# Moving three loads in a gated attention and mixer kernel: late v pieces of batch 1 at outputs 14 to 22, mixer weights V and U at outputs 11 and 13

## The chip, the cores and the metric

The kernel runs on one core of one Trainium2 chip. The metric is the device time of one execution in microseconds (us). Work is done by five engines with queues of their own: TensorE (PE; its weight loads are shown apart as PEld), VectorE (DVE), ScalarE (ACT), GpSimd (POOL) and SyncE (SP). In this kernel GpSimd and SP mostly issue DMA transfers; 16 DMA engines carry them all.

## The reference

For each of 8 batches (u and v are 3136 x 256, z is 3136 x 64, all float32), attention without softmax, gated by u, and then a mixer with a residual:

```
scores = (z @ z.T) / 3136
attn   = maximum(scores, 0) ** 2
x      = u * (attn @ v)                      # first part: gated attention

h      = x.T @ U @ V                         # U: 3136 x 32, V: 32 x 3136
y      = x + h.T
out    = y + maximum(y @ w_ch1, 0) @ w_ch2   # w_ch1: 256 x 1024, w_ch2: 1024 x 256
```

U, V, w_ch1 and w_ch2 are shared by all batches. The mixer of a batch needs the x of the whole batch.

## The kernel before

The 3136 rows are cut into 25 tiles of up to 128 rows (24 full, one of 64, tile 24). The attention matrix is symmetric, so only half of its blocks are computed: for row tile j, `A[j]` (line 129) holds 13 blocks, those of tiles j to j + 12, counted around. `score` (line 352) makes them: matmuls of z against z (line 359), Relu with the scale on ScalarE (line 372), squaring on VectorE (line 374), in bf16. The other half is had by transposing: `turn` (line 392) issues a DMA transpose on SP (line 394) that turns the 12 later blocks of `A[o]` into a *strip*, one of seven buffers. A strip is called here by its tile.

An *output* is one row tile of attn @ v. `attend_steps` (line 526) makes it: 25 blocks, each as two matmuls of 64 rows (line 472), 13 blocks from the A tiles and 12 from the strip. Outputs go in the order of tiles 12, 13, ... 24, 0, ... 11, and "output i" of a batch is the i-th of these (`turns`, line 132). Two outputs share an accumulator and a load of u (`load_u`, line 452, two buffers); when the second is done, `close_pair` (line 481) adds the halves (lines 486, 487) and multiplies by u on VectorE (line 502). In the first output of a pair, the block of tile 24 is also done for the second output, so the second output's strip is needed already at the end of the first.

Batch 0 begins without any A tile. `start_up` (line 768) makes outputs 0 to 7 in an order of its own: outputs 0 to 3 from blocks made on the spot, outputs 4 to 7 with the strips of tiles 16 to 19. From output 8 (tile 20) on, the main loop (line 957) runs one output after the other, and spreads score steps, for outputs to come and for the next batch, between its matmuls. Strips of batch 0 are issued as `first_turns` (line 920) and `lead` (line 944) say; outputs 17 and 18 of batch 0 (tiles 4 and 5) use two strips that ScalarE and VectorE make without a DMA (`rebuild_steps`, line 397). From batch 1 on the mixer of the batch before runs beside attention: `rank_sums` (line 563) is the first user of U, at output 0 of batch 1; `low_rank` (line 615), the up matmuls (line 654) and the down matmuls (line 701) follow. V is copied by VectorE from a staging place (`V_tmp`, line 120) to its own tile by the `puts` (line 940) at outputs 16 to 21 of batch 0 and at output 0 of batch 1.

The order of every engine's queue is the order in which the program is written: no scheduler moves anything. GpSimd's queue holds all loads that convert float32 to bf16. A GpSimd instruction that waits holds back all that stand behind it; one that has nothing to wait for goes out as soon as the one before it has. So a load that is written "after output 11" goes out when the loads written before it are out, not when output 11 is done.

v is double buffered by batch (`v_both`, line 126). It is loaded in nine pieces (`V_PARTS`, line 311): eight of three tiles, and tile 24. Before the change, batch 1's pieces are placed so: pieces 0 to 2 in the opening, behind w_ch1, U and V (line 796, `run(fetches)`); pieces 3 and 4 in the opening too, behind a one-column copy on GpSimd, `mark` (line 869), which waits for the strip of tile 19 to land; the piece of tile 24 at output 10; pieces 5, 6 and 7 at outputs 17, 20 and 22 (line 955). They are first read at output 0 of batch 1.

Of the kernel before, what the change touches and what calls it, by code (L numbers as in the profile page):

```python
# [8 lines left out]
BF16 = mybir.dt.bfloat16  # L9
# [9 lines left out]
def _spread(main, filler):  # L19

    n, m = len(main), len(filler)
    k = 0
    for i, step in enumerate(main):
        step()
        while k < m and (2 * k + 1) * n <= (i + 1) * 2 * m:
            filler[k]()
            k += 1
    for step in filler[k:]:
        step()


def _merge(*lists):

    keyed = [
        ((i + 0.5) / len(part), n, s)
        for n, part in enumerate(lists)
        for i, s in enumerate(part)
    ]
    return [s for _, _, s in sorted(keyed, key=lambda e: e[:2])]
# [3 lines left out]
def kernel(  # L43
# [11 lines left out]
    nc = tc.nc  # L55

    B, S, D = u.shape
# [3 lines left out]
    P = 128  # L61
# [12 lines left out]
    LEAD = FIRST + AHEAD  # L74
    NG = 4
# [5 lines left out]
    persist = ctx.enter_context(tc.tile_pool(name="persist", bufs=1))  # L81
# [11 lines left out]
    halves = [slice(h * ROWS, (h + 1) * ROWS) for h in range(2)]  # L93


    mark = persist.tile([P, 1], BF16, name="mark")
    sets = [[ps1_pool.tile([P, 512], FP32, name=f"ps{k}{h}") for h in range(2)] for k in range(2)]
    opened = [0]

# [32 lines left out]
    def turns(i):  # L132
        return (FIRST + i) % NT
# [9 lines left out]
    def rows(ap):  # L143
        return ap[: NF * P, :].rearrange("(p t) d -> p t d", t=NF)
# [10 lines left out]
    def bursts_at(b):  # L155

        at = {0: (NC - 1, NC)} if b > 1 else {}
        if b:
            at.update({6: (0, 1, 2), 13: (3, 4, 5)})
        if b == B - 1:  # L160
            at[17] = (NC - 1, NC)
        return at
# [52 lines left out]
    def load_z(b, parts):  # L215
        if b not in z_raw:
            z_raw[b] = stage.tile([P, NT + 1, dqk], BF16, name="z_c")
        z_c = z_raw[b]
        for t0, t1 in parts:
            pool_dma(out=z_c[:, t0:t1, :], in_=rows(z[b])[:, t0:t1, :])  # L220
            if t1 == NF:
                for r in halves:
                    pool_dma(out=z_c[r, NF, :], in_=z[b, NF * P :, :])
# [78 lines left out]
    def load_v(b, part):  # L302
        t0, t1 = part
        v_bf = v_both[b % 2]
        if t0 < NF:
            pool_dma(out=v_bf[:, t0:t1, :], in_=rows(v[b])[:, t0:t1, :])  # L306
        else:
            for r in halves:
                pool_dma(out=v_bf[r, NF, :], in_=v[b, NF * P :, :])

    V_PARTS = [(t, t + 3) for t in range(0, NF, 3)] + [(NF, NT)]
    WHOLE = ((0, NF),)

    def weight_steps():


        def first_w():
            pool_dma(out=w1_bf, in_=moe_w_ch1.rearrange("(t p) d -> p t d", p=P))

        def second_w():  # L320
            pool_dma(out=w2_bf, in_=moe_w_ch2.rearrange("(p t) d -> p t d", t=NH))

        def narrow():
            pool_dma(out=U_bf[:, :NF, :], in_=rows(moe_U))
            pool_dma(out=U_bf[:TAIL, NF, :], in_=moe_U[NF * P :, :])

        def fetch():
            pool_dma(out=V_tmp, in_=moe_V)

        def put(ta, tb):  # L330
            src = V_tmp[:, : NF * P].rearrange("r (p t) -> r t p", t=NF)
            nc.vector.tensor_copy(
                out=V_bf[:R, col(ta) : col(ta) + (tb - ta) * P].rearrange("r (t p) -> r t p", p=P),
                in_=src[:, ta:tb, :],
            )

        def put_tail():
            for c in (col(NF), col(NF) + TAIL):
                nc.vector.tensor_copy(out=V_bf[:R, c : c + TAIL], in_=V_tmp[:, NF * P :])

        def copies(n):
            nc.vector.tensor_copy(out=V_bf[n : 2 * n, :], in_=V_bf[:n, :])

        fetches = [first_w, narrow, fetch]
        third = FIRST // 2
        puts = [lambda t=t: put(t, t + third) for t in range(0, NF, third)]
        return fetches, second_w, puts + [put_tail], [lambda n=n: copies(n) for n in (R, 2 * R)]


    strips = {}  # L350
# [417 lines left out]
    def start_up():  # L768
# [4 lines left out]
            out=eye,  # L773
            in_=eye,
# [18 lines left out]
            load_u(0, o)  # L793
        if B > 1:
            load_z(1, WHOLE)
        run(fetches)
        if B > 1:
            for part in V_PARTS[:3]:
                load_v(1, part)
# [65 lines left out]
            if j <= some[-1]  # L865
        ]
        run(_merge(nxt[2:], own))
        if B > 1:
            nc.gpsimd.tensor_copy(out=mark, in_=strips[0, LEAD + NG - 1][:, 0, :1])
            for part in V_PARTS[3:5]:  # L870
                load_v(1, part)
        rest = [
            lambda pair=pair: make_stored(pair, LEAD + NG)
            for pair in zip(range(LEAD - 1, FIRST - NG, -2), range(LEAD - 2, FIRST - NG - 1, -2))
# [59 lines left out]
    def run(steps):  # L934
        for s in steps:
            s()

    fetches, second_w, puts, copies = weight_steps()
# [9 lines left out]
    for b in range(B):  # L948
        more = b + 1 < B
        begin = 0 if b else 2 * NG  # L950
        all_bursts.append(bursts_of(b))
        burst_at = bursts_at(b)
        v_in = list(V_PARTS) if more and b else []
        own = own_at if b else first_at
        v_at = dict(zip((17, 20, 22, 10), V_PARTS[5:]))
        ahead = dict(zip((2, 3, 4, 7, 10, 11, 14), range(NC)))
        for i in range(begin, NT):
            o = turns(i)
            fill = [s for key in own.get(i, ()) for s in score_steps(b, *key)]
            if b == 0 and i in first_new:  # L960
                fill += rebuild_steps(b, first_new[i])
            if b == 0 and i in first_more:
                fill.append(lambda args=first_more[i]: make_stored(*args))
            if b == 0 and i == begin:
                fill = panel + fill
            if more:
                coming = next_at if b else after_first
                fill += [s for key in coming[i] for s in score_steps(b + 1, *key)]
                if b and i == (1 if b > 1 else 5):
                    load_z(b + 1, WHOLE)  # L970
                if i == (7 if b > 1 else 11 - 2 * b):
                    turn_z(b + 1, (FIRST, NF))
                if i == (10 if b else 12):
                    turn_z(b + 1, (0, FIRST))
                if b == 0 and i == 14:
                    mirror_z((FIRST, NF))
                if i in (16, 18, 20) and v_in:
                    load_v(b + 1, v_in.pop(0))
                if b == 0 and i in v_at:
                    load_v(b + 1, v_at[i])  # L980
                if b == 0 and i == 15:
                    mirror_z((0, FIRST))
                    extend_z(b + 1)
            main = attend_steps(b, o)
            if b and i in ahead:
                at = 17 if (i + (i > FIRST)) % 2 == 0 else 12 if i == 7 else 9 if i == 3 else 10
                main.insert(at, lambda c=ahead[i]: low_rank(b - 1, c))
            _spread(main, fill)
            if b == 0 and i in first_turns:
                for t in first_turns[i]:  # L990
                    turn(b, t)
            else:
                now = b * NT + i
                for k in range(turned_to[0] + 1, min(now + lead(b, i), NT * B - 1) + 1):
                    turn(k // NT, turns(k % NT))
                    turned_to[0] = k
            if not more and i == NT - AHEAD:
                turn_x(b, 0)
            if b * NT + i in puts:
                puts[b * NT + i]()  # L1000
            if (b, i) == ((1, 1) if more or b else (0, 20)):
                second_w()
            if b and i == 0:
                ps = spare()[0]
                rank_sums(b - 1, ps)
                rank_close(b - 1, ps)
            for n in burst_at.get(i, ()):
                up, down = all_bursts[b - 1 if i else b - 2][n]
                if i and not more and n >= NC - 1:
                    late += up + down  # L1010
                    up, down = [], []

                steps = [down.pop(0)] if n == 4 and n == burst_at[i][0] else []
                steps += _merge(up, down)
                if more:
                    steps = _merge(steps, [lambda part=part: load_v(b + 1, part) for part in [v_in.pop(0)]])
                    if n == 3:
                        steps.insert(2, lambda: mirror_z((FIRST, NF)))
                        steps.insert(4, lambda: mirror_z((0, FIRST)))
                        steps.insert(6, lambda: extend_z(b + 1))  # L1020
                run(steps)
# [4 lines left out]
    b = B - 1  # L1026
# [46 lines left out]
```

## Time and profile before

| what | us |
|---|---|
| median of 3 runs | 995.64 |
| lowest and highest of them | 995.33, 1003.48 |
| the profiled execution | 995.98 |
| its span, first to last instruction | 994.3 |
| DVE and ACT busy in the span | 552.7, 615.5 |
| GpSimd busy in the span | 169.5 |
| DMA transposes of strips in the span | 194, of 5.5 from issue to landing (median) |
| loads of v in the span | 57 pieces of 192 KB, 4.5 from issue to landing (median) |

The profile is of one execution. A timeline line gives start, length, engine, line of the kernel, operation, what is written and read, shapes and count, and in brackets how long the engine had been idle and what released it. "SPq" and "POOLq" are the queues that issue DMAs. In the list of DMA issues, "us to landing" is from the issue to the semaphore that tells of the data's arrival.

### The profile page before, as it was taken

To read this page: it belongs to the slowest core of one execution; us is meant where nothing else is said; L and a number is where in the kernel's file an instruction comes from. 1 tells how busy PE (TensorE), PEld (TensorE's weight loads), DVE (VectorE), ACT (ScalarE), POOL (GpSimd) and SP (SyncE) were. 2 spreads that over 40 slices of the span, in tenths; PEclk is the share of its full clock that TensorE was granted. 3 is DMA by queue.
4 is the path that set the end of the run, shared out by engine and by line. 5 is a ranking of instruction groups with operands and counts; after the bars stand their busy time and mean duration, and the time that the engine had idled before them with its cause. 6 is when DMAs were issued, how large, how long until landed. Compare 5 with 4: busy or idle time off the path is not lost.

```text
span 994.3 us, 31019 instructions
## 1 busy us (share of the span) xinstructions
PE 978.9 (98%) x13632; PEld 815.5 (82%) x13672; DVE 552.7 (56%) x1025; ACT 615.5 (62%) x845; POOL 169.5 (17%) x317
## 2 busy tenths in 40 slices
PE   8899999999999999999999999999999999999998
PEld 6778878888788888788887888878888788788876
DVE  6779845567346574364653655546546466352342
ACT  8878764766647575475755757467574676643154
POOL 5111111112121111212112121121211201111000
PEclk9999999999999999999999999999999999999999
DMA  9999999899899998998989989889989796595443
GB/s 180 163 192 209 181 155 202 174 184 174 142 196 175 168 178 151 181 179 169 168 163 172 180 166 169 162 171 186 159 165 185 164 192 125 129 191 122 83 107 101
DMA packets 399976, 164.42 MB, mean 165 GB/s; under 512 B 375568, under 2 KB 384464, under 8 KB 399840
## 3 DMA queue, kind: packets, MB, share of 16 engines
q1 hardware_dynamic: 371520, 96.14, 61.5%
q0 software_dynamic: 28320, 66.28, 28.9%
q8 instruction: 107, 1.75, 0.8%
q14 instruction: 29, 0.24, 0.1%
HBM read 61.88 MB, written 25.69 MB: 88 GB/s over the span
## 4 chain that ended last, share of the span: by engine, by line
PE 95%; DMA 2%; DVE 1%; ACT 1%; issue 0%; POOL 0%; DVEq 0%; POOLq 0%
PE ps L472 51%; PE ps L701 17%; PE ps L654 17%; PE ps L359 7%; DMA strip<-A 1%; PE ps L622 1%; PE ps L512 1%; DMA v<-in_v_dram 1%; ACT A L372 1%; PE ps L567 1%; DVE A L374 0%; DMA out_dram<-o_sb 0%; DVE both L487 0%; ACT both L486 0%; DVE x_bf L502 0%
## 5 line engine op out<-in xcount | busy, mean ns | idle before, releaser
L372 ACT ACTIVATE A<-ps 128x832 bf16<-128x832 f32 (+9 forms) x481 | 358.4, 764 | 141.0 <-PE ps L359 135.6
L472 PE MATMUL ps<-v,A 64*128 64x256 bf16 x4988 | 341.2, 269 | 1.6 <-DVE A L374 1.1
L374 DVE TENSOR_TENSOR A<-A 128x832 bf16<-128x832 bf16 (+9 forms) x481 | 243.5, 523 | 135.4 <-ACT A L372 133.1
L472 PE MATMUL ps<-v,strip 64*128 64x256 bf16 x4420 | 310.3, 269 | 3.8 <-DMA strip<-A 3.0
L472 PEld LDWEIGHTS <-A 64*128 64x128 bf16 x4988 | 252.7, 94 | 40.0 <-issue 7.0
L672 ACT ACTIVATE relu_bf<-ps 128x1024 bf16<-128x1024 f32 (+2 forms) x208 | 188.3, 909 | 150.5 <-PE ps L654 144.7
L472 PEld LDWEIGHTS <-strip 64*128 64x128 bf16 x4420 | 227.6, 94 | 35.0 <-DMA strip<-A 4.6
L701 PE MATMUL ps<-w_bf,relu_bf 128*128 128x256 bf16 (+1 forms) x1600 | 201.4, 273 | 0.4
L654 PE MATMUL ps<-ut,w_bf 128*128 128x512 bf16 (+2 forms) x856 | 198.1, 353 | 1.7
L701 PEld LDWEIGHTS <-relu_bf 128*128 128x128 bf16 (+1 forms) x1600 | 153.0, 98 | 40.3 <-issue 4.9
L719 DVE TENSOR_TENSOR o_sb<-ps,x_bf 128x512 f32<-128x512 f32 (+2 forms) x81 | 54.8, 678 | 171.1 <-PE ps L701 166.1
L654 PEld LDWEIGHTS <-w_bf 128*128 128x128 bf16 x896 | 117.9, 144 | 37.4 <-issue 6.7
L359 PE MATMUL ps<-zT 64*128 64x416 bf16 (+8 forms) x812 | 134.8, 312 | 0.0
L456 POOL DMA_DIRECT2D u_sb<-in_u_dram x96 | 53.1, 554 | 444.4 <-DVE x_bf L502 426.3
L486 ACT COPY both<-ps 128x512 f32<-128x512 f32 (+1 forms) x104 | 59.0, 568 | 70.1 <-PE ps L472 64.0
L487 DVE TENSOR_TENSOR both<-ps,both 128x512 f32<-128x512 f32 (+1 forms) x104 | 69.3, 666 | 30.8 <-ACT both L486 30.2
L502 DVE TENSOR_TENSOR x_bf<-both,u_sb 128x512 bf16<-128x512 f32 (+1 forms) x104 | 69.8, 672 | 3.7
L636 DVE TENSOR_TENSOR x_bf<-ps,x_bf 128x512 bf16<-128x512 f32 (+1 forms) x112 | 65.5, 626 | 11.3 <-PE ps L622 11.2
L732 POOL DMA_DIRECT2D out_dram<-o_sb x66 | 36.1, 546 | 186.4 <-DVE o_sb L719 174.5
L359 PEld LDWEIGHTS <-zT 64*128 64x128 bf16 x812 | 46.3, 94 | 3.6
L719 DVE TENSOR_TENSOR both<-ps,x_bf 128x512 f32<-128x512 f32 (+1 forms) x24 | 15.0, 623 | 57.3 <-PE ps L701 57.3
L306 POOL DMA_DIRECT2D v<-in_v_dram x61 | 33.7, 556 | 3.9 <-issue 2.7
(65 smaller groups left out, 242.8 us busy)
## 6 DMA issues: line engine op xcount, KB each, us to landing
u_sb<-in_u_dram POOLq DMA_DIRECT2D x96, 256.0 KB, 4.2
out_dram<-o_sb POOLq DMA_DIRECT2D x66, 256.0 KB, 2.9
v<-in_v_dram POOLq DMA_DIRECT2D x57, 192.0 KB, 4.5
out_dram<-both POOLq DMA_DIRECT2D x18, 256.0 KB, 2.5
strip<-A SPq DMA_TRANSPOSE x194, 5.5
out_dram<-o_sb SPq DMA_DIRECT2D x11, 256.0 KB, 2.0
z_c<-in_z_dram POOLq DMA_DIRECT2D x7, 384.0 KB, 7.0
w_bf<-in_moe_w_ch_dram POOLq DMA_DIRECT2D x2, 512.0 KB, 7.6
```

The lines of the kernel that those rows point to most:

```text
L359: mm(out=ps[:, k, :n], lhsT=zT[halves[k], j + at[k], :], rhs=zT_flat[halves[k], c + at[k] * P : c + at[k] * P + n], start=True, stop=True,)
L372: nc.scalar.activation(out=dst, in_=src, func=AF.Relu, scale=sc)
L374: nc.vector.tensor_tensor(out=dst, in0=dst, in1=dst, op=ALU.mult)
L472: mm(out=acc[t0][h][:, (o - t0) * D : (o - t0 + 1) * D], lhsT=w[halves[h]], rhs=v_both[b % 2][halves[h], j, :], start=start, stop=stop, **kw,)
L486: nc.scalar.copy(out=both[:, :w], in_=banks[1][:, :w])
L487: nc.vector.tensor_tensor(out=both[:, :w], in0=banks[0][:, :w], in1=both[:, :w], op=ALU.add)
L502: nc.vector.tensor_tensor(out=x_at(b, t0, n), in0=split(both[:, :w]), in1=u_sb[:, :n, :].rearrange("p t (a c) -> p t a c", c=P), op=ALU.mult,)
L636: nc.vector.tensor_tensor(out=q, in0=split(ps[h][:, : len(ks) * D]), in1=q, op=ALU.add)
L654: mm(out=ps[i][:, :w] if apart else ps[:, i, :w], lhsT=w1_at[:, db, hp + i, :], rhs=uT[c][:, db, len(chunks[c]) * P - w :], start=(db == 0 ...
L672: nc.scalar.activation(out=relus[c][:, hp : hp + 2, :w], in_=ps[:, :, :w], func=AF.Relu)
L701: mm(out=ps[r, k * D : (k + 1) * D], lhsT=relus[c][:, ht, q : q + (TAIL if two else P)], rhs=w2_bf[:, ht, :], start=(ht < 1 + two), stop=( ...
L719: nc.vector.tensor_tensor(out=o_sb[:p].rearrange("p t (a c) -> p t a c", c=P), in0=split(ps[:p, k0 * D : (k + 1) * D]), in1=x_at(b, t, nk) ...
```

## The change

Pieces 3 and 4 leave the opening, and with them `mark`, its tile and its wait. The main loop loads pieces 3 to 7 at outputs 14, 16, 18, 20 and 22 of batch 0 instead of 5 to 7 at 17, 20 and 22; tile 24's piece stays at output 10. Of the three weight loads of the opening only w_ch1 stays; V (`fetches[2]`) is written after output 11 and U (`fetches[1]`, two loads) after output 13. Nothing is computed otherwise, and TensorE, ScalarE, VectorE and SP have the same instructions in the same order.

```diff
-    mark = persist.tile([P, 1], BF16, name="mark")
...
-        run(fetches)
+        fetches[0]()
...
-        if B > 1:
-            nc.gpsimd.tensor_copy(out=mark, in_=strips[0, LEAD + NG - 1][:, 0, :1])
-            for part in V_PARTS[3:5]:
-                load_v(1, part)
...
-        v_at = dict(zip((17, 20, 22, 10), V_PARTS[5:]))
+        v_at = dict(zip((14, 16, 18, 20, 22, 10), V_PARTS[3:]))
...
             _spread(main, fill)
+            if b == 0 and i in (11, 13):
+                fetches[2 if i == 11 else 1]()
```

Seen in GpSimd's queue, from the w_ch1 load on ("u" is a load of u, "v 3" a piece of batch 1's v):

```
before: w1, U, U tail, V, v 0, v 1, v 2, u, u, mark, v 3, v 4, u, u, v tile 24, u tail, u, u, u, v 5, u, u, v 6, u, v 7, ...
after:  w1, v 0, v 1, v 2, u, u, u, u, v tile 24, u tail, V, u, u, U, U tail, v 3, u, v 4, u, v 5, u, v 6, u, v 7, ...
```

## The prediction

> **What bounds the kernel now.** I read the first page, then the busy time by stretches of 10 us, then the waits of the one stretch that stands out, then the timelines of TensorE and GpSimd there, then the landings of the transposes.
>
> ```profile
> PE 978.9 (98%) x13632; PEld 815.5 (82%) x13672; DVE 552.7 (56%) x1025; ACT 615.5 (62%) x845; POOL 169.5 (17%) x317
> PE 95%; DMA 2%; DVE 1%; ACT 1%; issue 0%; POOL 0%; DVEq 0%; POOLq 0%
> ```
>
> TensorE is busy for 978.9 of 994.3 us and holds 95% of the chain. There are 15.4 us in all that an edit to loads could win, unless it slows TensorE itself. Columns below: stretch, length, busy us of PE, PEld, DVE, ACT, POOL, clock, DMA share, GB/s.
>
> ```profile
> 38.00:48.00 10.00, 8.06 (x131) 6.72 (x129) 7.83 (x17) 7.79 (x15) 3.45 (x7) 1.00 1.16 147
> 48.00:58.00 10.00, 7.75 (x128) 6.47 (x125) 5.58 (x13) 6.46 (x11) 1.06 (x2) 1.00 1.18 161
> 58.00:68.00 10.00, 10.00 (x183) 7.63 (x180) 7.60 (x16) 8.34 (x12) 0.72 (x2) 1.00 0.96 193
> 78.00:88.00 10.00, 10.00 (x176) 8.72 (x172) 8.88 (x17) 9.65 (x13) 1.50 (x3) 1.00 1.16 206
> ```
>
> From 38 to 58 us TensorE idles 1.94 + 2.25 = 4.19 us; from 58 us on it is full. The granted clock is 1.00 throughout. In the same 20 us the DMA engines move the least (147 and 161 GB/s against 193 to 206 later) while their share stays above 1: transfers in each other's way. The three long idles, in TensorE's timeline (idle and releaser in brackets):
>
> ```profile
> 47.71 0.28 PE L472 MATMUL ps<-v,strip 64*128 64x256 bf16 x1 [1.80 <-DMA strip<-A]
> ...
> 54.64 0.72 PE L472 MATMUL ps<-v,strip 64*128 64x256 bf16 x10 [1.23 <-DMA strip<-A]
> ...
> 57.15 0.28 PE L472 MATMUL ps<-v,strip 64*128 64x256 bf16 x1 [0.81 <-DVE z_c L246]
> ```
>
> All three are reads of a transposed strip. The third is put down to a VectorE copy that ended at 57.11, but that matmul reads strip 23, which landed at 57.11 too. Matching every strip's landing with the first weight load that reads it, strips 21, 22 and 23 have a slack of 0.04 us each (landings 47.66, 54.59, 57.11); no other strip of batch 0 has under 1.2 us. GpSimd's timeline at that place:
>
> ```profile
> 38.75 0.22 POOL L869 COPY mark<-strip 128x1 bf16<-128x1 bf16 x1 [9.62 <-DMA strip<-A]
> 38.98 1.08 POOL L306 DMA_DIRECT2D v<-in_v_dram  x2
> 42.20 0.55 POOL L456 DMA_DIRECT2D u_sb<-in_u_dram  x1 [2.14 <-DVE x_bf L502]
> 45.95 0.54 POOL L456 DMA_DIRECT2D u_sb<-in_u_dram  x1 [3.20 <-DVE x_bf L502]
> 46.48 1.07 POOL L309 DMA_DIRECT2D v<-in_v_dram  x2
> 54.10 1.06 POOL L459 DMA_DIRECT2D u_sb<-in_u_dram  x2 [6.55 <-DVE x_bf L502]
> ```
>
> The two v pieces of batch 1 go out at 38.98, in the instant in which strips 21 (issued 38.95) and 22 (40.92) do. How long strips then take, issue to landing: first the one issued at 37.07, before the pieces, then the five issued from 38 to 56 us.
>
> ```profile
> strip<-A SPq DMA_TRANSPOSE x1, 3.8
> ```
>
> ```profile
> strip<-A SPq DMA_TRANSPOSE x5, 8.7
> ```
>
> So a strip takes 3.8 us undisturbed and 8.7, 13.7, 10.0 and 7.8 us (strips 21 to 24) behind the pieces and what queues after them; strips 0 and 1, issued at 56.46 and 60.88, are at 3.8 again. (A strip has the number of its tile; 24 is followed by 0.)
>
> **The change part by part.** The order of TensorE, ScalarE, VectorE and SP is the same; only GpSimd's queue differs.
>
> *The two pieces at 38.98, gone.* Strip 21: source ready at 38.95, at 3.8 us it lands at 42.8. TensorE wants it at 47.71 - 1.80 = 45.9: the wait goes, 1.80 us. Strip 22: issued at 40.92; lands between 44.7 (3.8 us) and 46.8 (5.9 us, what the strip issued at 66.02 took with one u load in its way). TensorE now wants it at 54.64 - 1.23 - 1.80 = 51.6: 1.23 us gone. Strip 23: its source is squared at 45.57 + 1.22 = 46.8, so it is issued no earlier than the present 47.16 or 0.3 us before; it lands between 50.6 and 53.1, the second with the u load of 45.95 and the two small v pieces in its way. Wanted at 57.15 - 0.81 - 1.23 - 1.80 = 53.3: 0.81 us gone, with 0.2 to 2.7 us to spare. That is the tightest of the three. Bounds: both ends empty the wait; above them stands the 10.0 us of today (57.1), which would give back 3.8 us. I take the nearer rows. Sum: 1.80 + 1.23 + 0.81 = 3.84 us. The rest of the 4.19 (0.21 us of it a wait for ScalarE) stays.
>
> *mark, gone.* GpSimd's copy of 0.22 us and its wait of 9.62 us. Nothing is gained: the u load behind it waits 2.14 us more for VectorE's multiply anyway and stays at 42.20.
>
> *U and V out of the opening.* Three issues of about 0.54 us on GpSimd (at 16.39 to 17.43), landing 8.2 to 8.8 us later. Without them three v pieces land some us earlier than 27.3 to 30.0, and strips 16 to 19 earlier than 31.2 to 38.7. TensorE waits for none of these (slack 4.2, 2.1, 1.2, 1.7 us); its idles from 20 to 30 us are for ScalarE and VectorE. Cost and gain 0; the cover is the score work of TensorE, ScalarE and VectorE.
>
> *V at output 11.* GpSimd does not wait for output 11: it issues V behind the u tail of 54.10, at about 51.3 after the 2 to 3 us won before it. In the opening it took 8.8 us to land. First use: VectorE's copies at output 16, some 20 us later. Its price is what it does to strips 0, 1 and 2, which may take 8.3, 6.9 and 6.3 us (issue to first use) and take 3.8, 3.8 and 4.3 now. One u load added 2.1 us to a strip (5.9 - 3.8). I take 0 lost, since 4.3 + 2.1 is the only sum that comes over its room, by 0.1, and V has 2 to 3 us to pass before that strip is issued; bounds 0 and 13.7 - 6.3 = 7.4 us.
>
> *U and piece 3, then piece 4, at outputs 13 to 16.* They follow the u loads now at 67.85 and 71.93, so GpSimd issues U, its tail, piece 3, a u load and piece 4 within about 5 us. Strip 3 has 73.91 - 66.02 = 7.9 us and takes 5.9; the u load of 67.85 lands at 72.33, and U queues behind it on the same queue, so strip 3 (landed 71.93) is through before U moves. Strips 6 and 7 have 14.7 and 15.7 us; outputs 4 and 5 use strips that ScalarE makes. Nearest rows: 8.5 us for the strip beside a u load and one piece (72.5), 13.7 us for the worst beside two pieces and two u loads. Both are below 14.7: 0 lost. Bounds 0 and, for strip 3, 13.7 - 7.9 = 5.8 us. On GpSimd the four issues (about 2.2 us) go before u loads that wait for VectorE for 3.5 to 6.5 us anyway; the u load of 71.93 will queue behind U and piece 3 in the DMA engines, and the multiply that reads it comes 12 us after its issue (84.90 is released by it): hidden too.
>
> *Pieces 5 and 6 one or two u loads later; piece 7 where it was.* They are read in batch 1, from about 101 us; strips 8 to 15 have 8.8 to 13 us of slack. 0.
>
> *Weighing a page.* The Trainium skill, page "DMA: Bandwidth & Descriptors", section "Anatomy of one DMA", prices a transfer at about 2.0 us fixed and its bytes at 436 GB/s; by it the two pieces of 192 KB occupy the DMA engines for some 0.9 us (estimate), the strips come 0.9 us earlier and the gain would be 0.9 us, not 3.84. The rows speak against it: five strips lose 4 to 10 us each around those pieces. The same page's "Issuing engines are not separate DMA queues" says that all queues share 16 DMA engines and interleave; that speaks against this change wherever the pieces go next, and the 8.5 us of the strip at 70.96 agrees.
>
> **Sum.** The profiled execution took 995.98 us (span 994.3, 1.7 around it): 995.98 - 3.84 = 992.1. The median of the runs is 995.64, 0.34 lower; on that scale 991.8.
>
> **Rivals.**
> *Only the bytes count (part of the gain).* At the 206 GB/s of 78 to 88 us, two pieces of 192 KB are 1.9 us. Strips 21 to 23 land 1.9 us earlier, the first wait goes, and TensorE reaches the next ones 1.8 us earlier, so these stay: gain 1.9 us, 993.7. For it: the two u loads and the small v pieces remain in the same place. Against: 147 GB/s there, so the mix costs more than its bytes.
> *The transposes are slow by themselves (no effect).* SP spends 6.05, 4.32 and 4.77 us on issuing strips 22 to 24, against 1.3 to 2.5 for most. If that were its own doing, 995.6. Against: the strips issued at 20.22 and 26.60 took 6.33 and 3.87 us to issue as well, behind the opening's loads; the ones between and after did not.
> *The wait moves to strip 3 (slower).* If U and piece 3 reach the DMA engines before strip 3 is through, it takes 8.5 to 13.7 us against its room of 7.9: TensorE waits 0.6 to 5.8 us at output 16. At the far end 3.84 is paid back with 2.0 on top: 997.6. It decides above 7.9 + 3.84 = 11.7 us. For it: 13.7 has happened under two pieces and two u loads. Against: U stands behind a u load in the queue, and only one strip is exposed.
>
> **How the numbers follow.** All three waits go: 0.62 (990.8 to 992.8 with what one execution differs from another). Bytes alone: 0.18. No effect: 0.07. Strip 3, or strip 2 under V: 0.11. More than 4.2 us won: 0.02. The predicted time is the first case's, 991.8. From 990.5 to 996.0 the range takes in the first three; the slower case and what lies below stay out. One per cent is 10 us, about what a measurement of this kernel tells from no change; the whole idle of TensorE in the stretch is 4.2 us, so nearly all is "same": 0.97, faster 0.01, slower 0.02 (waits at several strips at once).
>
> **What would show it.** Right: TensorE full (10.00) in 48 to 58 us; no wait for a strip in batch 0; strips 21 to 23 landing in 4 to 6 us, and from there on everything about 3.8 us earlier. U, piece 3 and piece 4 should be seen to stretch strips 6 to 9 to 8 to 14 us with no wait. Wrong: a wait at strip 23, or new ones at strips 2, 3 or 6; strips 21 and 22 still over 8 us with no v piece beside them (the loads were not the cause).

## The result: 0.4% slower, and the profile after

| | before | after |
|---|---|---|
| median of 20 runs, us | 995.87 | 1000.6 |
| lowest and highest, us | 992.0, 1003.48 | 993.83, 1010.18 |
| the profiled execution, us | 995.98 | 1000.42 |
| its span, us | 994.3 | 998.6 |

The ratio after to before is 1.004, 95% interval 1.0022 to 1.0059 (disturbed executions are left out of ratios, not of medians). I had said 991.8, in a range of 990.5 to 996.0: the kernel became slower instead of faster, and the time lies above the range. Line numbers in the changed kernel are one lower than before (L472 is now L471, L456 is L455).

From the page of the changed kernel, the group of the matmuls that read strips (instructions | busy us, ns of one | idle just before them, and what ended it).

```profile
L471 PE MATMUL ps<-v,strip 64*128 64x256 bf16 x4420 | 311.2, 270 | 6.8 <-DMA strip<-A 6.8
```

6.8 us of waits for strips are there. The same stretches as before, and three of 4 us (columns as in the prediction):

```profile
38.00:48.00 10.00, 9.86 (x164) 8.79 (x161) 8.15 (x18) 8.92 (x16) 2.14 (x4) 1.00 0.97 170
48.00:58.00 10.00, 9.76 (x168) 7.67 (x164) 7.39 (x17) 8.70 (x15) 1.58 (x3) 1.00 1.29 145
58.00:68.00 10.00, 8.27 (x147) 6.52 (x148) 8.16 (x19) 5.81 (x11) 2.75 (x5) 1.00 1.24 182
68.00:72.00 4.00, 0.35 (x8) 0.07 (x2) 2.81 (x7) 0.72 (x2) 1.17 (x2) 1.00 1.29 101
72.00:76.00 4.00, 3.61 (x41) 2.68 (x42) 1.33 (x4) 2.09 (x6) 0.00 (x0) 0.61 1.29 139
```

From 38 to 58 us TensorE is nearly as full as forecast (0.38 us idle in place of 4.19). Then comes a hole that the kernel before did not have: 1.73 us of idle from 58 to 68, 3.65 of the next 4 us, and from 72 to 76 the granted clock is 0.61 in the mean (0.50 from 72.87 to 76.29 us, in the trace's record of the clock). TensorE's timeline there:

```profile
61.00 0.28 PE L471 MATMUL ps<-v,strip 64*128 64x256 bf16 x2 [0.71 <-DMA strip<-A]
...
65.26 0.28 PE L471 MATMUL ps<-v,strip 64*128 64x256 bf16 x2 [1.02 <-DMA strip<-A]
...
65.43 1.04 PE L471 MATMUL ps<-v,strip 64*128 64x256 bf16 x16
...
72.39 0.28 PE L471 MATMUL ps<-v,strip 64*128 64x256 bf16 x2 [4.04 <-DMA strip<-A]
...
72.73 1.76 PE L471 MATMUL ps<-v,strip 64*128 64x256 bf16 x16
...
78.44 1.48 PE L471 MATMUL ps<-v,strip 64*128 64x256 bf16 x24 [1.04 <-DMA strip<-A]
```

Strips 0, 1, 2 and 3 are all late: 0.71 + 1.02 + 4.04 + 1.04 = 6.81 us. The same 16 matmuls take 1.04 us at 65.43 and 1.76 us at 72.73, behind the long wait. GpSimd's timeline says what was issued:

```profile
51.41 1.07 POOL L458 DMA_DIRECT2D u_sb<-in_u_dram  x2 [4.46 <-DVE x_bf L501]
52.45 0.54 POOL L327 DMA_DIRECT2D relu_bf<-in_moe_V_dram  x1
...
63.12 0.54 POOL L455 DMA_DIRECT2D u_sb<-in_u_dram  x1 [3.58 <-DVE x_bf L501]
63.65 0.54 POOL L323 DMA_DIRECT2D U_bf<-in_moe_U_dram  x1
...
64.70 0.59 POOL L305 DMA_DIRECT2D v<-in_v_dram  x1
```

And the DMA issues of the microsecond 52 to 53 (KB, us from issue to landing):

```profile
relu_bf<-in_moe_V_dram POOLq DMA_DIRECT2D x1, 196.0 KB, 8.3
...
strip<-A SPq DMA_TRANSPOSE x1, 8.8
```

V goes out 0.26 us behind strip 0 (issued 52.19), and that strip takes 8.8 us where it took 3.8 before. What follows is late too: strips 1, 2 and 3 take 7.4, 9.1 and 13.3 us (3.8, 4.3 and 5.9 before). SP's queue is held up as well: issuing the transpose of z behind strip 0 takes it 3.94 us (1.54 before), and strip 3 goes out at 65.10, behind U and piece 3.

Matching every weight load of TensorE with its place in the program gives the difference of the two profiles step by step, after minus before: -0.6 us in the opening (the first v load landed 2.1 us earlier, though nothing ahead of it was changed), -4.7 at the first use of strip 23, -3.8 at strip 0, -2.6 at strip 1, +1.6 at strip 2, +4.5 at strip 3, and then unchanged to the end (+4.4). The gain came, a little over its size; 9.3 us were lost at strips 0 to 3. As the yardstick for the experiments I take the time from the first use of strip 23 to that of strip 6. With nothing late in it, it is 26.2 us; in after it is 35.4. By its parts (first use to first use): 23 to 0 8.59 (7.62 before), 0 to 1 4.26 (3.06), 1 to 2 7.13 (2.92), 2 to 3 6.05 (3.17), 3 to 6 9.34 (9.44). Of the 2.9 us that were added between strips 2 and 3, 1.04 are the wait and some 1.8 the lower clock (half the clock for 3.4 us, with TensorE busy all through, is 1.7).

### The profile page after: what moved, and what is told of

Same layout as the page of the kernel before. It is cut to its first block, busy times and chain, and to the rows that moved or that the text cites. A ratio compares the mean times of both kernels' runs of the same rounds, so it can differ in the third digit from the quotient of the medians.

```text
span 998.6 us, 31056 instructions
## 1 busy us (share of the span) xinstructions
PE 982.6 (98%) x13672; PEld 815.5 (82%) x13672; DVE 553.3 (55%) x1025; ACT 615.1 (62%) x845; POOL 169.3 (17%) x316
## 4 chain that ended last, share of the span: by engine, by line
PE 95%; DMA 2%; ACT 1%; DVE 1%; issue 0%; DVEq 0%
PE ps L471 50%; PE ps L653 17%; PE ps L700 17%; PE ps L358 7%; DMA strip<-A 2%; PE ps L621 1%; PE ps L511 1%; ACT A L371 1%; PE ps L566 1%; DVE A L373 0%; DMA out_dram<-o_sb 0%; PE ps L268 0%; ACT both L485 0%; DVE both L486 0%; DVE o_sb L718 0%
## 5 line engine op out<-in xcount | busy, mean ns | idle before, releaser
L471 PE MATMUL ps<-v,A 64*128 64x256 bf16 x4988 | 341.4, 269 | 1.3 <-DVE A L373 1.1
L471 PE MATMUL ps<-v,strip 64*128 64x256 bf16 x4420 | 311.2, 270 | 6.8 <-DMA strip<-A 6.8
L471 PEld LDWEIGHTS <-A 64*128 64x128 bf16 x4988 | 252.8, 94 | 40.3 <-issue 6.3
L471 PEld LDWEIGHTS <-strip 64*128 64x128 bf16 x4420 | 228.0, 94 | 38.9 <-DMA strip<-A 8.2
L653 PE MATMUL ps<-ut,w_bf 128*128 128x512 bf16 (+2 forms) x896 | 201.5, 355 | 0.0
L455 POOL DMA_DIRECT2D u_sb<-in_u_dram x96 | 53.2, 554 | 462.2 <-DVE x_bf L501 436.7
```

The lines of the kernel that those rows point to most:

```text
L471: mm(out=acc[t0][h][:, (o - t0) * D : (o - t0 + 1) * D], lhsT=w[halves[h]], rhs=v_both[b % 2][halves[h], j, :], start=start, stop=stop, **kw,)
L653: mm(out=ps[i][:, :w] if apart else ps[:, i, :w], lhsT=w1_at[:, db, hp + i, :], rhs=uT[c][:, db, len(chunks[c]) * P - w :], start=(db == 0 ...
```

## The experiments

Theory: a load of some 400 KB of float32, converted on the way, issued beside strip 0, makes that strip and the next ones come too late; V does it here, and any such load would. Rivals: it is V's form alone (rows of 3136 columns); it is U and pieces 3 and 4 at outputs 13 to 16; it is not the change at all but what one execution differs from another. Two starting points are used: the changed kernel, and "pieces late", which leaves U and V in the opening and puts the pieces at outputs 17 to 22. Edits are shown against the kernel that their first line names, or else against the changed one. The table has what was measured.

| run | what differs | median (us), before beside it | ratio, 95% | strip 23 to 6, profile |
|---|---|---|---|---|
| e1, e13 | U and V in the opening, pieces at 14 to 22 | 1004.65, 996.83; 992.74, 996.16 | 1.0035 (1.0000 to 1.0069); 0.9979 (0.9947 to 1.0011) | 26.2; 26.4 |
| e2 | pieces 3, 4 in the opening, V 11, U 13 | 997.14, 996.83 | 0.9997 (0.9972 to 1.0021) | 31.5 |
| e3, e11 | pieces late | 992.32, 996.83; 993.37, 995.52 | 0.9957 (0.9935 to 0.9979); 0.9997 (0.9961 to 1.0033) | 26.3; 26.6 |
| e4 | change with U 11, V 13 | 1000.24, 996.83 | 1.0009 (0.9982 to 1.0035) | 34.5 |
| e5 | pieces late, V 11 | 997.77, 995.23 | 1.0048 (1.0014 to 1.0082) | 29.5 |
| e6 | pieces late, second copy of V's bytes at 11 | 997.23, 995.23 | 1.0020 (0.9994 to 1.0046) | 32.4 |
| e7 | pieces late, U 21 | 1002.53, 995.23 | 1.0038 (1.0005 to 1.0072) | 26.2 |
| e10 | change with V in the opening | 1006.05, 995.52 | 1.0096 (1.0081 to 1.0111) | 26.2 |
| e14 | pieces late, U 13 | 995.7, 996.16 | 1.0002 (0.9968 to 1.0036) | 26.3 |
| e16 | pieces late, V 13 | 996.42, 993.64 | 0.9997 (0.9963 to 1.0031) | 26.5 |
| e17 | pieces late, U 11 | 994.6, 993.64 | 1.0029 (0.9992 to 1.0065) | 28.0 |
| e9, e15 | the change again | 997.85 (one run); 1001.45, 996.16 | none; 1.0067 (1.0041 to 1.0092) | 32.5; 33.1 |
| e8, e12 | before again | 992.12; 1016.36 (one run each) | none | 26.7; 26.3 |

### The two halves of the change (e1, e2)

```diff
# e1: U and V stay in the opening
-        fetches[0]()
+        run(fetches)
...
-            if b == 0 and i in (11, 13):
-                fetches[2 if i == 11 else 1]()
```

> V and U are back in the opening; pieces 3 to 7 stand at outputs 14 to 22 as in the change. Theory A (the pieces in the opening cost the waits at strips 21 to 23, and V at output 11 with U behind it costs the new waits at strips 0 to 3): the three first waits are gone, about 4 us won by strip 23; strips 0 and 1 on time; at strips 2 and 3 piece 3 alone may cost 0 to 1.5 us; 2.5 to 4 us faster than before. Rival B (pieces 3 and 4 at outputs 14 and 16 make the new waits): strips 2 and 3 wait 4 us and more together, no gain. Rival C (strips 0 to 3 cannot follow a TensorE that is 4.7 us earlier, whatever is loaded): waits at strips 0 to 3 of 7 to 9 us, about 4 us slower than before.

```diff
# e2, against before: only U and V are moved
-        run(fetches)
+        fetches[0]()
...
+            if b == 0 and i in (11, 13):
+                fetches[2 if i == 11 else 1]()
```

> Pieces 3 and 4 stay in the opening behind mark; V at output 11 and U at output 13 as in the change. Theory A: the waits at strips 21 to 23 stay (about 3.8 us), V and U bring new ones at strips 0 to 3 of 2 to 7 us: that much slower than before. Rival B: strips 0 to 3 on time, within 1 us of before. Rival C: as B, since TensorE is not early.

e1's profile has strips 0 to 3 at 3.8 to 6.2 us and no wait at them; its stretch is 26.2 us. So the pieces at 14 and 16 by themselves do not make strips 2 and 3 late. Its median is nevertheless high: in its profile strips 8 to 10 landed 13 to 21 us after their issue, and TensorE waited 7.2 us at strip 10. This did not come again in e13, below. The gain of 2.5 to 4 us that I had expected of e1 is not in its ratio. In e2's timeline of TensorE waits at strips 0, 1 and 2 are back, without any piece moved:

```profile
62.29 0.28 PE L472 MATMUL ps<-v,strip 64*128 64x256 bf16 x2 [1.04 <-DMA strip<-A]
...
67.29 0.28 PE L472 MATMUL ps<-v,strip 64*128 64x256 bf16 x2 [1.77 <-DMA strip<-A]
...
72.26 0.28 PE L472 MATMUL ps<-v,strip 64*128 64x256 bf16 x2 [1.87 <-DMA strip<-A]
```

The loss goes with U and V. Yet e2 is no slower than before in its ratio (its lowest time, 993.78 us, is 1.9 over that of before beside it): strip 23 was first used at 53.28 us in it, against 57.15 in before's first profile, with the two pieces still written where they had been. The waits at strips 21 to 23 that I had expected to stay had gone without the edit that was to remove them.

### Pieces late (e3), and U and V in each other's place (e4)

```diff
# e3: as e1, and
-        v_at = dict(zip((14, 16, 18, 20, 22, 10), V_PARTS[3:]))
+        v_at = dict(zip((17, 18, 19, 20, 22, 10), V_PARTS[3:]))
# e4: the change, with
-                fetches[2 if i == 11 else 1]()
+                fetches[1 if i == 11 else 2]()
```

> V and U in the opening; pieces 3 to 7 at outputs 17, 18, 19, 20 and 22, where strips have 8 us and more of slack. Theory A and rival B: strips 21 to 23 and 0 to 3 on time, no wait for a strip over 1 us: 3.5 to 4.5 us faster than before. Rival C: waits at strips 0 to 3 of 7 to 9 us, 4 us slower.

> As the change, with U at output 11 and V at output 13. If the shape of the V load is what costs (32 rows of 12.5 KB, against 128 of 3 KB for U, the same bytes), strips 0 and 1 wait 0 to 0.5 us, and V costs its time at strips 2 and 3: 5 us or more there. If the bytes are what costs, strips 0 and 1 wait 2.2 us together as in the change, and strips 2 and 3 about 7: the time of the change within 1 us.

e3 is the fastest of this group, 0.9957 of before; its strips 0 to 3 take 3.8 to 5.5 us. In e4 U at output 11 stretches strip 0 to 8.2 us as V did, but TensorE waits only 0.22 us for it; strips 0 and 1 cost less than the 2.2 us that I had expected if the bytes alone count. The long wait is at strip 3 now (issued 63.16), with V and piece 3 issued right behind it (63.85 and 64.36), so that it takes 11.6 us. TensorE's timeline, and the clock after the wait:

```profile
74.83 2.74 PE L471 MATMUL ps<-v,strip 64*128 64x256 bf16 x24 [4.40 <-DMA strip<-A]
```

```profile
76.00:80.00 4.00, 4.00 (x44) 2.92 (x42) 1.73 (x6) 1.25 (x3) 0.06 (x1) 0.50 1.24 126
```

That is the third rival of the prediction (a load and piece 3 in the way of strip 3) with V in U's place: 4.4 us of wait and, at half the clock, 2.8 us more before strip 6.

### One load at output 11 (e5, e6, e17)

```diff
# e5: e3 with V at output 11
-        run(fetches)
+        run(fetches[:2])
...
+            if b == 0 and i == 11:
+                fetches[2]()
# e17: e3 with U at output 11
-        run(fetches)
+        fetches[0]()
+        fetches[2]()
...
+            if b == 0 and i == 11:
+                fetches[1]()
# e6: e3, and V's bytes once more, as 128 rows of 784, into a tile that is free then
+            if b == 0 and i == 11:
+                flat = w2_bf.rearrange("p h d -> p (h d)")[:, :784]
+                pool_dma(out=flat, in_=moe_V.rearrange("r (q c) -> (r q) c", q=4))
```

> As the kernel with late pieces (pieces 3 to 7 at outputs 17 to 22, 0.9957 of before), with V alone moved from the opening to output 11. Theory A1 (V's load makes the waits at strips 0 and 1): strip 0 takes 8 to 9 us and strip 1 about 7 us from issue to landing, TensorE waits 1 and 1.2 us there, strips 2 and 3 are on time; the time is 2 us over that of the kernel with late pieces, ratio about 0.998. Rival (V only hurts together with the loads behind it): no wait over 0.3 us, ratio 0.995 to 0.996.

> As the kernel with late pieces, with V in the opening and one more load at output 11: the same 401 KB of V once more, laid out as 128 rows of 3 KB, into a tile that is not in use yet (it computes nothing and is overwritten later). If the 32 long rows of V's own load are what is dear, this costs like a v piece: strips 0 and 1 take 5 to 6 us and nothing waits, ratio 0.995 to 0.996. If the bytes are: as V alone at output 11, waits of 2 us in all, 0.998.

> As the kernel with late pieces, with U alone moved from the opening to output 11 (behind the u load of tile 24, beside strip 0). If the place makes the cost, strips 0 to 2 wait 1.5 us and more together, as with V there (3.4); best executions at 993 and over. If V's load makes it, they wait under 0.5 us and the best executions are near 991.5.

TensorE's timeline of e5, and the strip among its DMA issues from 52 to 53 us:

```profile
61.15 0.28 PE L471 MATMUL ps<-v,strip 64*128 64x256 bf16 x2 [0.57 <-DMA strip<-A]
...
65.42 0.28 PE L471 MATMUL ps<-v,strip 64*128 64x256 bf16 x2 [1.03 <-DMA strip<-A]
...
69.66 0.28 PE L471 MATMUL ps<-v,strip 64*128 64x256 bf16 x2 [1.14 <-DMA strip<-A]
```

```profile
strip<-A SPq DMA_TRANSPOSE x1, 8.4
```

The same of e17, with U in V's place:

```profile
60.94 0.28 PE L471 MATMUL ps<-v,strip 64*128 64x256 bf16 x2 [0.79 <-DMA strip<-A]
...
67.74 0.28 PE L471 MATMUL ps<-v,strip 64*128 64x256 bf16 x2 [0.65 <-DMA strip<-A]
```

```profile
strip<-A SPq DMA_TRANSPOSE x1, 8.7
```

V alone makes strip 0 take 8.4 us and costs 3.2 us (29.5 - 26.3), with a wait at strip 2 that I had not expected and a ratio of 1.0048 where I had expected 0.998; U alone 8.7 us and 1.7 us (1.44 us of waits, just under the 1.5 that I had set for "the place"). In e6, V's bytes in 128 rows made strips 0 to 2 take 7.8, 8.6 and 8.1 us; its stretch is not counted, as that was the slowest execution of this kernel (1007.23 us). So V's form is not needed: each such load beside strip 0 more than doubles that strip's time. Whether the form adds to the cost is not shown, nor whether the conversion or the bytes read are what matters, since no load without conversion was put there. In whole times, the lowest of each against the lowest of the kernel before beside it, V's cost is seen, U's hardly, and e6's not: 994.03 and 991.98 us in e5, 992.77 and 991.96 in e17, 991.45 and 991.98 in e6; without such a load (e3) 991.22 and 991.89.

### The same loads two outputs later (e14, e16), and at 21 (e7)

```diff
# e14: e3 with U at output 13 (e7: with "i == 21")
-        run(fetches)
+        fetches[0]()
+        fetches[2]()
...
+            if b == 0 and i == 13:
+                fetches[1]()
# e16: e3 with V at output 13
-        run(fetches)
+        run(fetches[:2])
...
+            if b == 0 and i == 13:
+                fetches[2]()
```

> As the kernel with late pieces, with U alone moved from the opening to output 13. If U there makes strip 2 or 3 late by itself, as V at output 11 does with strips 0 to 2, they wait 1 to 3 us and the ratio is 0.998 to 1.002; if U needs the pieces behind it for that, strips 2 and 3 wait under 0.5 us and the ratio is 0.994 to 0.998.

> As the kernel with late pieces, with V alone moved from the opening to output 13 (behind two u loads). If the place makes the cost, strips 0 to 3 wait under 1 us in all, as with U alone at output 13; best executions near 991.5 us. If V's load makes it wherever it stands, strips 2 and 3 wait 1.5 us and more and the best executions are at 993 and over.

> As the kernel with late pieces, with U moved from the opening to output 21 (first read at output 0 of batch 1). Theory A: the opening gets lighter and nothing is lost at output 21, where strips have 8 us and more of slack: as fast as the kernel with late pieces or up to 1 us faster, ratio 0.994 to 0.996. Rival (any further load between 60 and 100 us makes strips late): 0.998 and more.

The stretch from 58 to 68 us and strip 0 (DMA issues of 52 to 53 us) in e14:

```profile
58.00:68.00 10.00, 9.99 (x187) 8.57 (x186) 9.62 (x24) 7.85 (x15) 2.75 (x5) 1.00 1.11 206
```

```profile
strip<-A SPq DMA_TRANSPOSE x1, 3.8
```

and the stretch in e16:

```profile
58.00:68.00 10.00, 9.94 (x180) 8.28 (x181) 9.62 (x23) 7.66 (x14) 2.39 (x5) 1.00 1.09 195
```

Where V or U goes out alone after output 13, strip 0 takes 3.8 us in both, TensorE is full (the changed kernel has 8.27 there), and the stretch is 26.3 and 26.5 us. The lowest times agree: 991.25 us in e14 and 990.81 in e16, against 992.39 and 991.96 of the kernel before beside them; the ratios (1.0002, where I had expected 0.994 to 0.998, and 0.9997) show neither gain nor loss. The place decides, not the load: behind output 11 it meets strip 0, which has 8 us, and holds up all that comes after. What it is about the place is only partly known. In e16 V goes out between strips 3 and 6 and these take 6.9 and 6.6 us (5.5 and 5.1 in e3), 1.4 and 1.6 us more, where strip 0 took 4.6 more. At output 11 the load goes out 0.3 us behind the strip, in e16 1.2 us behind one and 0.5 ahead of the other; no run moves that distance alone. e7's profile has no wait at strips 0 to 3 either; its strips of tiles 17 and 18 were late in the opening, where nothing differs from e3 but U's absence, and a transpose of x in batch 1 (`ut`) made TensorE wait 3.3 us. Its lowest time, 990.64 us, is the lowest of all runs, and its median 1002.53; the ratio, 1.0038, is not the 0.994 to 0.996 that I had expected, and why is not known.

### V alone back in the opening (e10), and repetitions (e8, e9, e11, e12, e13, e15)

```diff
# e10: the change without V at output 11
         fetches[0]()
+        fetches[2]()
...
-            if b == 0 and i in (11, 13):
-                fetches[2 if i == 11 else 1]()
+            if b == 0 and i == 13:
+                fetches[1]()
```

> The change with V alone put back into the opening (U at output 13, pieces at outputs 14 to 22). Theory (a load beside strip 0 is what costs): strips 0 and 1 on time; U and piece 3 may still make strips 2 or 3 wait 0.5 to 3 us; faster than the change by 2 us or more, ratio to before 0.998 to 1.002. Rival (U and the pieces behind it are the whole cost): the time of the change, 1.003 to 1.005.

> The kernel before once more, for a second profile of it. If the waits at strips 21 to 23 belong to the kernel, they are there again with 3 to 5 us in all; if they were that execution's, they are under 1.5 us.

> The changed kernel once more, for a second profile. If the waits at strips 0, 1 and 2 belong to the loads at outputs 11 and 13, they are there again (strips 0 and 1: 1.5 to 3.5 us together; strip 2 and what follows: 2 us and more); if they were that execution's, strips 0 to 2 have 2 us of slack and more.

> The kernel with late pieces once more (V and U in the opening; pieces 3 to 7 at outputs 17, 18, 19, 20 and 22). If its gain is real, the ratio is 0.994 to 0.998 again and its best runs are near 991.3 us; if it was chance, 0.999 to 1.002. In its profile strips 0 to 3 are on time.

> The kernel before, a third profile. The first had 3.8 us of waits at strips 21 to 23, the second 0.8 at all strips. If the large ones are the rule, 3 us and more again; if they come and go with the execution, anything from 0 to 4.

> V and U in the opening, pieces 3 to 7 at outputs 14 to 22, once more. Theory (the pieces every second output from 14 on leave the DMA engines no room, and strips 7 to 10 become late once nothing holds TensorE back before): strips 0 to 3 on time, strips 7 to 10 with under 4 us of slack or with waits; ratio 1.000 to 1.008. Rival (the first run's late strips 8 to 10 were that execution's): slack over 5 us at strips 6 to 10, ratio 0.995 to 0.999.

> The changed kernel, a third profile and more times. Strips 0 and 1 wait 1.5 to 2.5 us together, strip 2 and what follows 2 to 7; the ratio is 1.002 to 1.006.

In e10 strips 0 to 3 take 3.8, 4.0, 4.7 and 6.7 us and none is waited for, with U, its tail and piece 3 where the changed kernel has them: the whole loss at strips 0 to 3 hangs on V at output 11. But strips 8 to 10 were late in this profile (strip 8 took 16.8 us), and none of its four executions was under 1004 us, so that the ratio is 1.0096 where I had expected 0.998 to 1.002; in e14, with U at 13 and the pieces later, strip 8 took 6.4 us. e1, with the pieces at 14 to 22 and U in the opening, had the same late strips, and e13, the same kernel as e1, had about 6 us of slack and more at strips 7 to 10. Whether U and pieces 3 and 4 close together do that or something outside the kernel is not settled.

The change again, e9 at strip 2 in TensorE's timeline, then its clock from 68 to 76 us:

```profile
70.48 0.40 PE L471 MATMUL ps<-v,strip 64*128 64x256 bf16 x2 [2.60 <-DMA strip<-A]
```

```profile
68.00:72.00 4.00, 1.52 (x16) 1.12 (x18) 2.40 (x7) 0.91 (x3) 1.17 (x2) 0.76 1.27 209
72.00:76.00 4.00, 4.00 (x65) 3.38 (x63) 1.81 (x6) 1.63 (x5) 0.00 (x0) 0.81 1.24 152
```

e9 waited 0.14, 1.14 and 2.60 us at strips 0, 1 and 2; e15 1.23 us at strip 0, 3.04 at strip 2 and 0.47 at strip 3: at strips 0 and 1 a little less than expected. Three profiles of the changed kernel show strip 0 at 8.8, 7.9 and 9.2 us and a stretch of 35.4, 32.5 and 33.1 us: a loss in each. That is the change's own; e15's ratio, 1.0067, is a little over the range that I had set. The gain is not as steady. The kernel before, in e8, its stretches and its one longer wait from 38 to 62 us:

```profile
38.00:48.00 10.00, 9.25 (x151) 7.66 (x148) 7.76 (x17) 8.35 (x15) 2.14 (x4) 1.00 1.19 203
48.00:58.00 10.00, 9.79 (x172) 8.15 (x167) 7.29 (x17) 8.85 (x15) 1.05 (x2) 1.00 1.07 172
```

```profile
43.59 0.39 PE L472 MATMUL ps<-v,strip 64*128 64x256 bf16 x4 [0.61 <-DMA strip<-A]
```

0.96 us of idle where the first profile had 4.19, and the longer wait is at strip 20. What differs can be read in GpSimd's queue, here e8's:

```profile
36.37 0.32 POOL L869 COPY mark<-strip 128x1 bf16<-128x1 bf16 x1 [7.64 <-DMA strip<-A]
36.63 1.07 POOL L306 DMA_DIRECT2D v<-in_v_dram  x2
```

The two pieces wait in `mark` for strip 19. In e8 that strip landed at 36.31 us, the pieces went out beside strip 20, and strips 20 to 23 took 6.9, 7.5, 5.9 and 5.6 us; in the first profile it landed at 38.70, and the pieces met strip 21 and stood ahead of strip 22 (13.7 us). e2 (36.87) is like e8, and e12 (37.40) lies between, with strips 21 to 23 at 9.8, 10.3 and 6.4 us. So the waits that I had counted seem to hang on how long the opening takes; four profiles go that way, and no run moves that landing alone.

Strip 23 is first used at 57.15, 53.03 and 56.56 us in the three profiles of before; at 52.2 to 53.1 us in thirteen of the fifteen profiles that have no pieces 3 and 4 in the opening (54.56 in e6, which began 1.7 us late, and 57.42 in e7). So moving the pieces wins 0 to 5 us, by the execution; in the mean of the three profiles (55.6) against a typical 52.6 it is 3.0 us, and 2.5 without e12, whose execution took 1016.36 us. The change's three stretches cost 9.2, 6.3 and 6.9 us over 26.2, 7.5 in the mean. The difference, +4.5 us (+5.0 without e12), stands beside the measured ratio, whose 1.004 is 4.0 us (2.2 to 5.9). e12 shows how far a wait can go in TensorE's timeline:

```profile
128.21 1.04 PE L472 MATMUL ps<-v,strip 64*128 64x256 bf16 x8 [10.61 <-DMA strip<-A]
```

That is the unchanged kernel. Such spells came in e1, e10 and e12 at strips, in e3, e7 and e13 at `ut`, the transpose of x in batch 1.

*The best version.* Pieces late (e3, e11) beat the changed kernel in both measurements (0.9957 and 0.9997 of before, against 1.004 and 1.0067). Against before one is clear (0.9957) and one is not (0.9997). The lowest times, 990.8 to 991.3 us in e3, e11, e13 and e14 against 991.7 to 992.4 of the kernel before beside them, suggest that about 1 us is won when nothing else is late.

## Why the prediction was wrong

*The two pieces at 38.98, gone: right in kind, its size that of one execution.* Strips 21, 22 and 23 landed in 5.5, 5.0 and 6.1 us (I said 4 to 6), the waits went (strip 23 landed 0.04 us before its use, just in time), and TensorE stood 4.7 us earlier at strip 23 (I said 3.8; 0.6 came from the opening). But e8 and e2 keep the pieces and have strip 23 at 53.0 and 53.3 us: 3.84 us was what that one profile held. That profile was the only one when I forecast, and I took its waits for the kernel's. Strip 22's 13.7 us was 5.9 and 10.3 in the two other profiles of before. (The prediction counts five slow strips there; the view with x5 takes in strip 20, at 3.8 us, so there are four, with a median of 9.3 and not 8.7.)

*mark, and U and V out of the opening: 0.* Right for the waits: none there in the profiled pair, before or after. But `mark` also sets when the two pieces go out, and this step did not ask what that does.

*V at output 11: this step failed.* "I take 0 lost", by the row of one u load that added 2.1 us to a strip. Measured: strip 0 took 8.8 us where it had 8.1, and V alone costs 3.2 us (e5). The rows for a better choice were in the prediction: V's own 8.8 us of landing in the opening, and four strips at 7.8 to 13.7 us beside two pieces of about the same size. A u load lands as the float32 that it reads; V is converted, and lands at 196 KB, a v piece at 192: that row was nearer in kind. Two more points of that step were wrong. I had V go out 2 to 3 us ahead of a strip (the sentence speaks of strip 2, but its numbers fit strip 0 alone); but strip 0's issue moved by 4.3 us (56.46 to 52.19) and V's place by 2.7 (the end of the u tail's issue, 55.16 to 52.45), so that the two met. And each strip was weighed by itself, while a late strip is followed by late ones: the upper bound, 7.4 us at one strip, was passed by the sum over four, 9.2 us, of which 6.8 were waits.

*U and piece 3, then piece 4: 0.* Right at strip 3 without V ahead (e14 with U, e1 and e13 with the pieces, e10 with both, none with a wait there), wrong behind V: strip 3 then took 13.3, 7.6 and 11.7 us in the three profiles of the change. The bound I had put there was 13.7. I had strip 3 through before U moves; so it is in e14, where it goes out 2.4 us ahead of U, but behind V it went out at 65.10, after U (63.65) and piece 3 (64.70). With the loads in each other's place (e4) TensorE waited 4.4 us at strip 3. Strips 6 to 9 had no wait, as forecast, but only strip 6 was stretched to the 8 to 14 us that I had named: they took 8.4, 7.3, 4.6 and 6.4 us.

*The price of a wait.* I counted waits at their length. Behind the 4.04 us at strip 2 TensorE ran at half its clock for 3.4 us: 1.8 us more in after, 1.4 in e9 and, at strip 3, 2.8 in e4. This term was not in the sum at all.

*Sum, after the fact, for the profiled pair:* -0.6 (opening) - 4.1 (strips 21 to 23) + 6.8 (waits at strips 0 to 3) + 1.8 (clock) + 0.5 (the rest between strip 23 and strip 6, not traced) = +4.4; the spans differ by 4.3.

*The rivals.* "The wait moves to strip 3", which the chances name "strip 3, or strip 2 under V", had the sign and the kind of loss, with 0.11. It named the wrong load and place: U and piece 3 do nothing to strip 3 without V (e10), and the first strip to be late is 0. Its price was too low because it let one strip be late. "Only the bytes count" falls in the profiled pair: the gain by strip 23 was 4.1 us and not 1.9; at strip 0, 196 KB at 206 GB/s are 1 us, and the strip lost 5. "The transposes are slow by themselves" falls there too (strips 21 to 23 came early with the pieces gone); but e8, with the pieces in and little wait, shows that the pieces alone do not make the loss either.

*The weighed page.* By the Trainium skill, page "DMA: Bandwidth & Descriptors", section "Anatomy of one DMA", the estimate for the pieces had been 0.9 us; the runs have 0 to 5. The warning drawn from "Issuing engines are not separate DMA queues" (the Trainium skill, "DMA: Bandwidth & Descriptors"), that a load moved elsewhere meets other transfers there, is what happened at strip 0: 8.8 us instead of 3.8. It did not hold wherever a load went: at output 13, V or U alone cost nothing at strips 0 to 3 (e14, e16).

## What to carry to other kernels

Before a load is moved, look at what is issued in the same microsecond and what room that has, and price the load by the row of a transfer of its own size and form beside the same kind of neighbour; let the upper end of that row into the sum, since the same load cost one strip 4.6 us and others 1.5. A stall that stands in one profile may be that execution's own: profile the kernel several times before counting its waits as a gain. Price a long wait of TensorE at more than its length, and let one late transfer make the next ones late too.

## What the runs showed of the hardware

*The clock falls behind a long wait.* The granted clock is 1.00 all through 58 to 68 us in e5, with waits of 0.57 and 1.03; it is 0.76 in 68 to 72 and 0.81 in 72 to 76 us around a wait of 2.60 us (e9), 0.61 in 72 to 76 behind 4.04 us (after), 0.50 in 76 to 80 behind 4.40 us (e4). In the trace's record of the clock each fall ahead of the last matmul is to 0.50 and lasts 3.41 us or a multiple of it (after 3.41, e4 6.83, e12 20.48). At that clock 16 matmuls took 1.76 us instead of 1.04. The Trainium skill, page "TensorE: Matmul & The Clock Gate", section "What's actually happening", says that TensorE falls to half its clock after an idle window of some 3.4 us and needs as much of busy time to be at full again. The runs agree on the half and on 3.4 us of slow work. The idle time before a fall is not fixed in them: a wait of 2.07 us brought one (e16, at 129.11 us), one of 3.62 us did not (e1, at 140.90 us).

*A transpose and a large converting load issued together do badly.* Strip 0, at 3.8 us without, took 7.8 to 9.2 us in all eight profiles with such a load issued 0.3 us behind it, whether V, U or V's bytes in another shape. Beside strips 3 and 6 (e16) V added 1.4 and 1.6 us only.

*Long transposes.* Every profile has at least one transpose of over 10 us behind the first 60 us. Spells of them that make TensorE wait came in some executions of several versions, before included (up to 26.5 us in e12). What starts them stays open.
